# Retention decay put on the values and on a chunk's result, in an attention, routing and FFN kernel on one core

## The chip, the cores and the metric

The kernel runs on one core of a Trainium2 chip. The metric is the device time of one execution in microseconds, lower is better. Three executions of the kernel before took 1035.68, 1039.04 and 1039.63 us, a median of 1039.04 us.

## What is computed

Three layers follow each other. The first is attention with a decaying state, for 4 batches, 8 heads, 768 tokens and a head size of 64; gamma differs from head to head:

```
gamma = 1.0 - 2.0 ** (-5.0 - arange(H))
for t in range(S):
    state = gamma * state + k[t] outer v[t]
    y[t] = (1 / sqrt(D)) * q[t] @ state
```

The second gives each of the 3072 rows to one of 8 experts (384 rows each, by a gate product with `w_gate` and a greedy order over all logits) and applies `relu(x @ w1) @ w2` of that expert. The third is `softplus(x @ w_in) @ w_out`.

## The kernel before

**Stages.** From 0 to about 128 us runs the attention (class `Attn`), with the gate's logits beside it; then the routing of the first expert (class `Route`), until about 164 us; then the two FFN layers expert by expert (class `Ffn`), to the end. The change touches the attention and what is interleaved with it; routing and FFN keep their code.

**Chunks.** The attention works on 24 chunks of 128 tokens, six to a batch. In a chunk no token loop is left: the decay is written as powers of gamma. For a chunk j with place c in its batch (c = j mod 6), TensorE does, in this order within iteration j of `emit`:

- `qk(j+1)` (line 125): scores of the next chunk, keys against queries, into `pA`. VectorE then multiplies `pA` by the table `cm` and writes `at` (line 126). `cm` holds the causal mask, 0.125 and gamma to the power of the distance within a chunk, a plane of its own for each head: 128x1024.
- `xo(j-1)` (line 164): transposes the result `yT` of the chunk before and takes its product with `w_gate`, in one matmul against `rx` (an identity matrix beside the gate's columns), into `pX`. ScalarE copies the rows to `xs` (line 168), SyncE stores them to `xd` (line 178), VectorE sums the gate's parts (`gate`, line 173).
- `y(j)`: where c > 0, the decayed queries `qs` against the state `sb` (line 138), and in all chunks the values against `at` (line 142), both into `pY`. ScalarE copies `pY` to `yT` (line 145).
- `kv(j)` (line 155): where c < 5, the keys against the decayed values `vh`, added into the state `pS`. ScalarE copies it to `sb` (line 157).

`scale` (line 106) makes `qs` on GpSimd: the queries times the table `gqt`, which is loaded in five pieces of 256 KB, one ahead of the queries of each of the chunks 1 to 5 (line 98). `scale_v` (line 114) makes `vh` on ScalarE: eight products, one for each head, with a power of gamma that falls with t; where c = 5 it makes none.

**Interleaved work.** `Conv` turns `w_in` into a high and a low part (16 tiles of 512 KB). Each tile takes three ScalarE instructions (lines 241, 243, 269), three of VectorE (256, 258, 264) and two of GpSimd (242, 259). `side(j, part)` is called three times in an iteration and says how many of its 50 steps shall be done by then; before, this starts in chunk 1, and `cv.ahead()` issues four raw tiles ahead of the loop. After every sixth chunk `R.first_part` puts a list of 12 short VectorE instructions (lines 383 to 399) into the loop, the routing's first look at six chunks of logits.

**What sets the order.** The order is written out by hand in `emit`; each engine takes its instructions strictly in program order. All the big loads are on SyncE's queue in program order: queries with keys (`qk_t`, 512 KB a chunk, four buffers), keys with values (`kv_t`, the same), raw tiles (five buffers), and the stores of `xd`. A load waits until its buffer's last reader is done and, as the queue's rows name it, for an earlier transfer with the same semaphore lane. The PSUM tiles `pA`, `pY`, `pX` have one buffer each: `qk(j+2)` can't write `pA` before `at` of chunk j+1 is made.

Of the kernel before, what the change touches and what calls it, by code (L numbers as in the profile page):

```python
# [20 lines left out]
def shape_tables(H, S):  # L21


    g = 1.0 - 2.0 ** (-5.0 - np.arange(H, dtype=np.float64))
    i = np.arange(128)
    t = i[:, None] + 128 * np.arange(S // 128)
    gk = g ** (-t[:, :, None].astype(np.float64))
    m = np.where(i[:, None] <= i, 0.125 * g[:, None, None] ** (i - i[:, None]).clip(0), 0.0)
    m = m.reshape(H // 2, 2, 128, 128).transpose(2, 1, 0, 3).reshape(128, -1)
    tab = np.concatenate([np.eye(128), m, gk.reshape(128, -1)], axis=1)  # L30
    gq = 0.125 * g[:, None] ** np.arange(S, dtype=np.float64)
    gq = np.repeat(gq.reshape(H // 2, 2, 1, S // 128, 128), 64, axis=2)
    gq = gq.transpose(1, 2, 3, 0, 4).reshape(128, -1)
    return tab.astype(np.float32), gq.astype(np.float32)
# [19 lines left out]
class Attn:  # L54
# [4 lines left out]
    def __init__(self, tc, ctx, ps, qk, kv, w_gate, tab, gqt, ident, L, xd, B, H, S):  # L59
# [34 lines left out]
    def load(self, j, which=("qk", "kv")):  # L94
        for n in (which,) if isinstance(which, str) else which:
            t = self.t[n, j] = self.ld.tile([128, 2, 512], FT, name=n + "_t", bufs=4)
            if n == "qk" and 0 < j < self.NC:
                self.nc.sync.dma_start(self.gq[:, j - 1], self.gq_in[:, j * 512:(j + 1) * 512])
            self.nc.sync.dma_start(t, (self.qk_in if n == "qk" else self.kv_in)[j])

    def scale(self, j):

        c, nc = j % self.NC, self.nc
        if c:
            qs = self.t["qs", j] = self.wk.tile([128, self.HP, 128], FT, name="qs", bufs=2)
            nc.gpsimd.tensor_mul(qs.rearrange("p a t -> p (a t)"), self.t["qk", j][:, 0], self.gq[:, c - 1])

    def scale_v(self, j):

        c, nc = j % self.NC, self.nc  # L110
        if c < self.NC - 1:
            vh = self.t["vh", j] = self.wk.tile([128, self.H, 64], FT, name="vh", bufs=2)
            for h in range(self.H):
                nc.scalar.activation(vh[:, h], self.t["kv", j][:, 1, h * 64:h * 64 + 64], AF.Copy,
                                     scale=self.gk[:, c, h:h + 1])
# [12 lines left out]
    def y(self, j):  # L128
        nc, c = self.nc, j % self.NC
        pY = self.ps.tile([128, 2, 512], FT, name="pY")  # L130
        at, v = self.t["at", j], self.t["kv", j][:, 1]
# [12 lines left out]
        yT = self.t["yT", j] = self.wk.tile([128, 2, 2, 128], FT, name="yT")  # L144
        nc.scalar.activation(yT, pY[:, :, 0:256].rearrange("p b (k t) -> p b k t", k=2), AF.Copy)
# [13 lines left out]
    def xo(self, j):  # L159
# [7 lines left out]
        xs = self.wk.tile([128, 2, 2, 128], FT, name="xs", bufs=3)  # L167
        nc.scalar.activation(xs, pv[:, :, :, 0:128], AF.Copy)
        self.t["xs", j] = xs
        self.t["pv", j] = pv  # L170

    def gate(self, j):
        self.nc.vector.tensor_reduce(self.L[:, j, :], self.t.pop(("pv", j))[:, :, :, 128:136].rearrange("p b a e -> p e b a"),
                                     axis=AX.XY, op=OP.add)
# [6 lines left out]
    def emit(self, side, logits):  # L181
# [3 lines left out]
        self.scale(1)  # L185
        self.late_constants()
        for j in range(n):
# [5 lines left out]
            side(j, 0)  # L193
            if j:
                self.xo(j - 1)
            self.y(j)
            side(j, 1)
            if j:
                self.gate(j - 1)
# [3 lines left out]
            if j + 2 < n:  # L203
                self.scale(j + 2)
# [7 lines left out]
        self.gate(n - 1)  # L212
# [8 lines left out]
class Conv:  # L221
# [673 lines left out]
def model(ctx, tc, qk, kv, w_gate, w1, w2, w_in, w_out, tab, gqt, out, B, H, S):  # L895
# [31 lines left out]
    cv.ahead()  # L927
# [44 lines left out]
```

## Time and profile before

| | us |
|---|---|
| median of three executions | 1039.04 |
| the profiled execution's own time | 1039.39 |
| its span, first to last instruction | 1037.6 |
| TensorE busy | 994.5 (96%) |
| VectorE busy | 636.3 (61%) |
| ScalarE busy | 585.0 (56%) |
| GpSimd busy | 186.1 (18%) |
| bytes read and written in HBM | 83.73 and 12.58 MB |

The shares are means over stages with different limits, so a stage is read by the view of its stretch and by what ended the waits there. L125 is line 125 of the kernel above; a row of the timeline gives the start, the duration, the engine, the line, the operation with its tiles, how many were merged, and in brackets the idle time ahead of it and what ended it. TensorE's matmuls in float32 are shown as two records each, so 8 matmuls read as x16.

### The profile page before, as it was taken

The numbers are of one execution on the slowest core, as the hardware profiler recorded it, in microseconds if no ns is written. First come the engines' busy times: TensorE is split into PE (matmuls) and PEld (weight loads), VectorE is DVE, ScalarE is ACT, GpSimd is POOL, SyncE is SP. The second block draws the span as 40 slices with busy tenths as digits, with TensorE's granted clock in tenths as the row PEclk, the third lists the DMA queues.
The fourth block names the chain that finished last, engine by engine and source line by source line (L and its number), as shares of the span: only waits on it lengthen the run. The fifth ranks groups of instructions, "written<-read, shape, count | busy, mean of one in ns | idle before, by whom it ended". The sixth has DMA issues, their size and how long they took to land.

```text
span 1037.6 us, 19094 instructions
## 1 busy us (share of the span) xinstructions
PE 994.5 (96%) x7266; PEld 901.9 (87%) x7266; DVE 636.3 (61%) x1649; ACT 585.0 (56%) x1245; POOL 186.1 (18%) x204
## 2 busy tenths in 40 slices
PE   5999878999999999999999999999999999999997
PEld 4888757978899889988998889888989899999996
DVE  3686687888766666766575567555665644454432
ACT  4897723676645563566446644665356546654664
POOL 4685422556210101010101010100010020001001
PEclk9998999999999999999999999999999999999999
DMA  9998434423141104110321023101410160014000
GB/s 358 401 405 306 146 96 137 128 82 112 54 142 32 31 21 124 50 31 11 117 67 32 11 92 92 31 1 52 122 32 1 52 192 1 1 41 123 1 1 31
DMA packets 41179, 97.55 MB, mean 94 GB/s; under 512 B 5376, under 2 KB 5504, under 8 KB 41088
## 3 DMA queue, kind: packets, MB, share of 16 engines
q1 hardware_dynamic: 36432, 83.12, 24.1%
q0 software_dynamic: 3840, 12.59, 3.7%
q8 instruction: 57, 0.93, 0.4%
q10 hardware_dynamic: 816, 0.63, 0.2%
q14 instruction: 34, 0.28, 0.1%
HBM read 83.73 MB, written 12.58 MB: 93 GB/s over the span
## 4 chain that ended last, share of the span: by engine, by line
PE 72%; issue 12%; POOL 5%; DVE 5%; DMA 2%; ACT 2%; another core or an unknown queue 0%; SPq 0%; ACTq 0%; POOLq 0%
PE h L659 11%; PE h L662 11%; PE h L660 10%; PE acc L757 7%; PE acc L762 7%; PE acc L758 7%; PE acc L651 3%; PE acc L653 3%; PE acc L652 3%; PE pX L164 2%; POOL wol L259 2%; PE pA L125 2%; POOL cA L242 2%; PE pY L142 2%; PE rt L406 2%
## 5 line engine op out<-in xcount | busy, mean ns | idle before, releaser
L723 DVE SCALAR_TENSOR_TENSOR gf<-h,sp 128x384 f32<-128x384 f32 x128 | 71.2, 556 | 185.2 <-ACT sp L721 185.0
L659 PE MATMUL h<-x2h,wih 128*128 128x384 f32 x512 | 176.5, 345 | 2.0 <-DVE xl L647 2.0
L660 PE MATMUL h<-x2h,wil 128*128 128x384 f32 x512 | 173.3, 338 | 0.0
L757 PE MATMUL acc<-whi,gh 128*128 128x512 f32 x384 | 153.2, 399 | 0.0
L758 PE MATMUL acc<-wlo,gh 128*128 128x512 f32 x384 | 151.2, 394 | 0.0
L719 ACT ACTIVATE sp<-h 128x384 f32<-128x384 f32 x128 | 62.6, 489 | 137.5 <-PE h L662 127.2
L643 ACT ACTIVATE h1h<-h 128x384 fp32r<-128x384 f32 x64 | 31.5, 492 | 148.8 <-PE h L662 105.5
L770 POOL DMA_INDIRECT out_dram<-rows,ix x24 | 25.3, 1053 | 501.4 <-ACT rows L768 498.0
L662 PE MATMUL h<-x2l,wih 128*128 128x384 f32 x512 | 112.8, 340 | 0.8 <-DVE x2l L647 0.6
L762 PE MATMUL acc<-whi,gl 128*128 128x512 f32 x384 | 111.2, 396 | 0.8 <-DVE gl L737 0.8
L659 PEld LDWEIGHTS h<-x2h,wih 128*128 128x128 f32 x512 | 96.6, 189 | 5.8 <-DVE xl L647 2.2
L660 PEld LDWEIGHTS h<-x2h,wil 128*128 128x128 f32 x512 | 96.6, 189 | 3.4
L662 PEld LDWEIGHTS h<-x2l,wih 128*128 128x128 f32 x512 | 92.1, 189 | 2.9 <-DVE x2l L647 2.9
L637 DVE TENSOR_TENSOR wlo<-wraw,whi 128x512 fp32r<-128x512 f32 x128 | 86.3, 689 | 6.1 <-ACT whi L636 6.1
L659 PE MATMUL h<-xh,whi 128*128 128x384 f32 x256 | 89.0, 348 | 0.7 <-ACT xh L646 0.7
L637 DVE TENSOR_TENSOR wlo<-wol,whi 128x512 fp32r<-128x512 f32 x128 | 89.0, 698 | 0.9 <-ACT whi L636 0.9
L651 PE MATMUL acc<-h1h,whi 128*128 128x384 f32 x256 | 88.4, 345 | 0.0
L762 PEld LDWEIGHTS acc<-whi,gl 128*128 128x128 f32 x384 | 72.0, 188 | 18.6 <-DVE gl L737 1.4
L660 PE MATMUL h<-xh,wlo 128*128 128x384 f32 x256 | 86.8, 339 | 0.0
L636 ACT ACTIVATE whi<-wraw 128x512 fp32r<-128x512 f32 x128 | 76.6, 624 | 17.1 <-DMA wraw<-in_moe_w_dram 14.2
L653 PE MATMUL acc<-h1l,whi 128*128 128x384 f32 x256 | 86.1, 336 | 0.0
L652 PE MATMUL acc<-h1h,wlo 128*128 128x384 f32 x256 | 86.1, 336 | 0.0
(201 smaller groups left out, 1932.1 us busy)
## 6 DMA issues: line engine op xcount, KB each, us to landing
wraw<-in_moe_w_dram SPq DMA_DIRECT2D x128, 256.0 KB, 2.7
qk_t<-in_qk_dram SPq DMA_DIRECT2D x24, 512.0 KB, 8.8
kv_t<-in_kv_dram SPq DMA_DIRECT2D x24, 512.0 KB, 6.4
raw<-in_moe_w_in_dram SPq DMA_DIRECT2D x16, 512.0 KB, 7.0
raw<-in_moe_w_out_dram SPq DMA_DIRECT2D x32, 256.0 KB, 2.8
xd<-xs SPq DMA_DIRECT2D x24, 256.0 KB, 4.7
gqt<-in_gqt_dram SPq DMA_DIRECT2D x5, 256.0 KB
ctab<-in_tab_dram ACTq DMA_DIRECT2D x1, 536.0 KB
```

Of the source, the lines that this page charges most:

```text
L636: nc.scalar.activation(hi, raw, AF.Copy)
L637: nc.vector.tensor_tensor(lo, raw, hi.bitcast(FT), op=OP.subtract)
L651: nc.tensor.matmul(ps, wh, ah, start=start, stop=False)
L652: nc.tensor.matmul(ps, wl, ah, start=False, stop=False)
L653: nc.tensor.matmul(ps, wh, al, start=False, stop=stop)
L659: mm(ps, wh(d), ah[:, d], start=d == 0, stop=False)
L660: mm(ps, wl(d), ah[:, d], start=False, stop=False)
L662: mm(ps, wh(d), al[:, d], start=False, stop=d == 3)
L723: nc.vector.scalar_tensor_tensor(g, ps, 0.0, a, op0=OP.max, op1=OP.add)
L757: nc.tensor.matmul(ps, gh[:, s], wh, start=f == 0, stop=False)
L758: nc.tensor.matmul(ps, gh[:, s], wl, start=False, stop=False)
L762: nc.tensor.matmul(ps, gl[:, s], wh, start=False, stop=f == 15)
```

## The change

The decay is split another way. With t = 128 c + i, gamma^(t-s) is gamma^(128 c) gamma^i on a row of the result times gamma^(-s) on a row of the values.

- The scores are multiplied by a plain causal mask, one 128x128 plane read for all eight heads, instead of the eight planes of `cm`. The table loaded with it shrinks from 1072 to 176 columns.
- `vh` is used for the product with `at` too, and is made for every chunk (c = 5 included), with three buffers instead of two.
- The queries go into the state product as they were loaded; `scale`, `qs` and the five loads of `gqt` are gone.
- The copy of `pY` to `yT` becomes a product with a table of factors, on VectorE instead of ScalarE. A table of 532 columns is loaded once; from it VectorE makes the factors of the chunks 1 to 5 with four instructions each, in the iterations before they are used.
- The gate's sum stands ahead of the copy of the rows, and `xo(j-1)` ahead of the first `side` of an iteration.
- No raw tile of `w_in` is issued ahead of the loop. Four are issued one by one, at the three `side` calls of chunk 1 and the first of chunk 2; the steps start in chunk 3 and are spread over the 63 calls from there.

```diff
-    m = np.where(i[:, None] <= i, 0.125 * g[:, None, None] ** (i - i[:, None]).clip(0), 0.0)
-    tab = np.concatenate([np.eye(128), m, gk.reshape(128, -1)], axis=1)
...
+    tab = np.concatenate([np.eye(128), i[:, None] <= i, gk.reshape(128, -1)], axis=1)
+    gq = np.concatenate([gs.reshape(128, -1), (0.125 * gb[:, :, None] ** i).reshape(128, -1)], axis=1)
...
+        self.gb = c.tile([128, gqt.shape[1]], FT, name="gqb")
         self.load(0, "qk")
         nc.scalar.dma_start(ct, tab[:, 128:])
+        nc.scalar.dma_start(self.gb, gqt)
         self.load(0, "kv")
...
-            if n == "qk" and 0 < j < self.NC:
-                self.nc.sync.dma_start(self.gq[:, j - 1], self.gq_in[:, j * 512:(j + 1) * 512])
...
-    def scale(self, j):
-        c, nc = j % self.NC, self.nc
-        if c:
-            qs = self.t["qs", j] = self.wk.tile([128, self.HP, 128], FT, name="qs", bufs=2)
-            nc.gpsimd.tensor_mul(qs.rearrange("p a t -> p (a t)"), self.t["qk", j][:, 0], self.gq[:, c - 1])
+    def factors(self, c):
+        n = (self.NC - 1) * 4
+        if 0 < c < self.NC:
+            for i in range(4):
+                s, k = slice(i * 128, i * 128 + 128), (c - 1) * 4 + i
+                self.nc.vector.tensor_scalar(self.gq[:, c - 1, s], self.gb[:, n:][:, s], self.gb[:, k:k + 1], None,
+                                             op0=OP.mult)
+        return self.gq[:, c - 1] if c else self.gb[:, n:]
...
-        if c < self.NC - 1:
-            vh = self.t["vh", j] = self.wk.tile([128, self.H, 64], FT, name="vh", bufs=2)
+        vh = self.t["vh", j] = self.wk.tile([128, self.H, 64], FT, name="vh", bufs=3)
...
-        nc.vector.tensor_mul(at, pA, self.cm)
+        nc.vector.tensor_tensor(at.rearrange("p s a t -> p (s a) t"), pA.rearrange("p s a t -> p (s a) t"),
+                                self.cm[:, None, :].to_broadcast([128, self.H, 128]), op=OP.mult)
...
-                    nc.tensor.matmul(to(hp, s), self.sb[j % 2][r, hp, :], self.t["qs", j][r, hp, :],
+                    nc.tensor.matmul(to(hp, s), self.sb[j % 2][r, hp, :], qt[r, hp, :],
...
-            nc.tensor.matmul(to(hp, s), v[:, h * 64:h * 64 + 64], at[:, s, hp, :],
+            nc.tensor.matmul(to(hp, s), vh[:, h], at[:, s, hp, :],
...
-        nc.scalar.activation(yT, pY[:, :, 0:256].rearrange("p b (k t) -> p b k t", k=2), AF.Copy)
+        nc.vector.tensor_tensor(yT, pY[:, :, 0:256].rearrange("p b (k t) -> p b k t", k=2),
+                                self.factor[c].rearrange("p (b k t) -> p b k t", b=2, k=2), op=OP.mult)
...
+        nc.vector.tensor_reduce(self.L[:, j, :], pv[:, :, :, 128:136].rearrange("p b a e -> p e b a"),
+                                axis=AX.XY, op=OP.add)
+        xs = self.t["xs", j] = self.wk.tile([128, 2, 2, 128], FT, name="xs", bufs=3)
         nc.scalar.activation(xs, pv[:, :, :, 0:128], AF.Copy)
...
     def side(j, part):
-        if j:
-            cv.step((3 * j - 2 + part) * 50 // 69)
+        n = 3 * j + part
+        if n >= 3:
+            cv.begin()
+        if n >= 9:
+            cv.step((n - 8) * 50 // 63)
...
-    cv.ahead()
     a.emit(side, logits)
```

How the instructions move is seen at three places. The first is the head of SyncE's queue, before the change (`qk_t` and `kv_t` are a chunk's loads, `gqt` a piece of the old table, `raw` a raw tile of `w_in`):

```order
L99 DMA qk_t<-in_qk_dram 128x1024
L99 DMA kv_t<-in_kv_dram 128x1024
L98 DMA gqt<-in_gqt_dram 128x512
L99 DMA qk_t<-in_qk_dram 128x1024
L99 DMA kv_t<-in_kv_dram 128x1024
L98 DMA gqt<-in_gqt_dram 128x512
L99 DMA qk_t<-in_qk_dram 128x1024
L99 DMA kv_t<-in_kv_dram 128x1024
L230 DMA raw<-in_moe_w_in_dram 128x1024 x4
L98 DMA gqt<-in_gqt_dram 128x512
L99 DMA qk_t<-in_qk_dram 128x1024
```

The same queue with the change:

```order
L98 DMA qk_t<-in_qk_dram 128x1024
L98 DMA kv_t<-in_kv_dram 128x1024
L98 DMA qk_t<-in_qk_dram 128x1024
L98 DMA kv_t<-in_kv_dram 128x1024
L98 DMA qk_t<-in_qk_dram 128x1024
L98 DMA kv_t<-in_kv_dram 128x1024
L98 DMA qk_t<-in_qk_dram 128x1024
L98 DMA kv_t<-in_kv_dram 128x1024
L98 DMA qk_t<-in_qk_dram 128x1024
L228 DMA raw<-in_moe_w_in_dram 128x1024 x2
```

The queries and keys of chunk 3 were the last of these rows, behind three pieces of `gqt` and four raw tiles; now they are the seventh, and the raw tiles come after those of chunk 4.

The second place is ScalarE from the making of `vh` (line 114 before, 115 after) through the two chunks behind it, in the second batch. Before:

```order
L114 ACTIVATE vh<-kv_t,ctab 128x64 x8
L168 ACTIVATE xs<-pX 128x512
L145 ACTIVATE yT<-pY 128x512
L269 ACTIVATE wih<-cA 128x4x128
L157 ACTIVATE sb_169<-pS 128x256
L114 ACTIVATE vh<-kv_t,ctab 128x64 x8
L241 ACTIVATE cA<-raw 128x512
L243 ACTIVATE cB<-raw 128x512
L168 ACTIVATE xs<-pX 128x512
L145 ACTIVATE yT<-pY 128x512
L157 ACTIVATE sb_168<-pS 128x256
```

With the change:

```order
L115 ACTIVATE vh<-kv_t,ctab 128x64 x8
L272 ACTIVATE wih<-cA 128x4x128
L174 ACTIVATE xs<-pX 128x512
L244 ACTIVATE cA<-raw 128x512
L246 ACTIVATE cB<-raw 128x512
L161 ACTIVATE sb_168<-pS 128x256
L115 ACTIVATE vh<-kv_t,ctab 128x64 x8
```

The copy to `yT` has left the queue, and `vh` is now what the line of `y` waits for, not only that of `kv`.

The third place is VectorE around the first list of the routing (its last row is G) and the two products to `at` behind it. Before:

```order
L399 TENSOR_TENSOR G<-kx,thr_85 128x276
L258 TENSOR_SCALAR cA<-cA 128x512
L126 TENSOR_TENSOR at<-pA,ctab 128x1024
L264 TENSOR_TENSOR wil<-cA,wih 128x4x128
L173 TENSOR_REDUCE L<-pX 128x8
L256 SCALAR_TENSOR_TENSOR cB<-raw,cB 128x512
L126 TENSOR_TENSOR at<-pA,ctab 128x1024
```

With the change:

```order
L402 TENSOR_TENSOR G<-kx,thr_85 128x276
L259 SCALAR_TENSOR_TENSOR cB<-raw,cB 128x512
L127 TENSOR_TENSOR at<-pA,ctab 128x1024
L171 TENSOR_REDUCE L<-pX 128x8
L261 TENSOR_SCALAR cA<-cA 128x512
L148 TENSOR_TENSOR yT<-pY,gqt 128x512
L267 TENSOR_TENSOR wil<-cA,wih 128x4x128
L127 TENSOR_TENSOR at<-pA,ctab 128x1024
```

The product to `yT` stands between two products to `at`, behind a step of the conversion; the gate's sum (`L<-pX`) comes right behind `at` and waits for TensorE, where it waited for ScalarE before.

## Rows read from the trace of the kernel before

**Rows 1.** Stages: stretch, length, busy (instructions) by engine, granted clock, DMA share, GB/s
```profile
0.00:26.00 26.00, 14.34 (x158) 13.03 (x159) 8.64 (x31) 12.77 (x36) 10.74 (x23) 0.91 0.96 358
26.00:52.00 26.00, 25.11 (x391) 21.84 (x392) 15.95 (x35) 21.89 (x62) 16.58 (x13) 0.96 1.03 401
52.00:78.00 26.00, 24.15 (x394) 21.19 (x390) 21.12 (x36) 24.77 (x75) 20.77 (x15) 1.00 1.03 406
78.00:104.00 26.00, 24.25 (x343) 21.48 (x344) 15.84 (x24) 18.49 (x53) 14.29 (x11) 0.87 0.85 306
```
**Rows 2.** Timeline of the first chunks, VectorE and TensorE
```profile
8.48 1.23 DVE L126 TENSOR_TENSOR at<-pA,ctab 128x1024 f32<-128x1024 f32 x1 [5.29 <-PE pA L125]
10.24 2.08 PE L125 MATMUL pA<-qk_t 64*128 64x128 f32 x16 [1.80 <-DMA qk_t<-in_qk_dram]
14.76 1.16 PE L125 MATMUL pA<-qk_t 64*128 64x128 f32 x16
22.63 2.08 PE L125 MATMUL pA<-qk_t 64*128 64x128 f32 x16 [3.50 <-DMA qk_t<-in_qk_dram]
```
**Rows 3.** Chain that ended last, in the attention: start, us, what
```profile
29.48 1.09 PE pA L125 x16
...
87.04 1.09 PE pA L125 x16
...
89.26 0.60 PE pY L138 x16
...
90.88 0.46 PE pS L155 x16
91.34 1.09 PE pA L125 x16
...
118.27 1.09 PE pA L125 x16
```
**Rows 4.** Waits from 0 to 190 us: engine line, for whom: total, times, longest
```profile
PE pA L125 <- DVE at L126: 5.8, 3, 3.6
```
**Rows 5.** Timeline around the second list of the routing
```profile
75.09 2.50 POOL L106 TENSOR_TENSOR qs<-qk_t,gqt 128x512 f32<-128x512 f32 x2
75.18 1.20 DVE L394 SCALAR_TENSOR_TENSOR kf<-sg,unas 128x6 f32<-128x6 int32 x1
...
79.75 2.08 PE L125 MATMUL pA<-qk_t 64*128 64x128 f32 x16 [3.59 <-DVE at L126]
```
**Rows 6.** Timeline of the attention's end and the last list, from 127.9 us
```profile
127.90 0.60 ACT L168 ACTIVATE xs<-pX 128x512 f32<-128x512 f32 x1 [1.28 <-PE pX L164]
128.53 0.19 DVE L173 TENSOR_REDUCE L<-pX 128x8 f32<-128x32 f32 x1 [3.38 <-ACT xs L168]
128.75 0.20 DVE L383 TENSOR_REDUCE m<-L 128x6 f32<-128x48 f32 x1
...
130.10 0.17 DVE L394 SCALAR_TENSOR_TENSOR kf<-sg,unas 128x6 f32<-128x6 int32 x1
...
130.51 0.30 DVE L399 TENSOR_TENSOR G<-kx,thr 128x276 bf16<-128x276 f16 x1
```
**Rows 7.** Timeline of ScalarE through one chunk with a whole tile of the conversion
```profile
34.42 0.38 ACT L157 ACTIVATE sb<-pS 128x256 f32<-128x256 f32 x1
34.68 2.01 ACT L114 ACTIVATE vh<-kv_t,ctab 128x64 f32<-128x64 f32 x8
...
38.74 0.59 ACT L145 ACTIVATE yT<-pY 128x512 f32<-128x512 f32 x1
39.22 0.38 ACT L157 ACTIVATE sb<-pS 128x256 f32<-128x256 f32 x1
```
**Rows 8.** Groups by line and shape, 0 to 170 us: busy us, mean ns
```profile
L106 POOL TENSOR_TENSOR qs<-qk_t,gqt 128x512 f32<-128x512 f32 x20 | 27.6, 1388 | 12.4 <-DMA qk_t<-in_qk_dram 9.6 <-issue 1.6 <-PE pY L138 1.2
...
L647 DVE TENSOR_TENSOR xl<-h,xh 128x512 fp32r<-128x512 f32 x3 | 2.1, 692 | 2.1 <-ACT xh L646 2.1
```
**Rows 9.** One line's instructions, line 264: duration in ns, shortest, median, longest
```profile
L264 DVE TENSOR_TENSOR wil<-cA,wih x15: 678/684/1760, 31.8 to 121.2; 128x512 fp32r<-128x512 f32 x15
```

More of the change, by code (lines that the diff above doesn't have):

```diff
@@ L27, in shape_tables @@
     gk = g ** (-t[:, :, None].astype(np.float64))
-    m = np.where(i[:, None] <= i, 0.125 * g[:, None, None] ** (i - i[:, None]).clip(0), 0.0)
-    m = m.reshape(H // 2, 2, 128, 128).transpose(2, 1, 0, 3).reshape(128, -1)
-    tab = np.concatenate([np.eye(128), m, gk.reshape(128, -1)], axis=1)
-    gq = 0.125 * g[:, None] ** np.arange(S, dtype=np.float64)
-    gq = np.repeat(gq.reshape(H // 2, 2, 1, S // 128, 128), 64, axis=2)
-    gq = gq.transpose(1, 2, 3, 0, 4).reshape(128, -1)
+    heads = np.array([[[4 * k + 2 * (s ^ b) + s for k in range(H // 4)] for s in range(2)] for b in range(2)])
+    gb = np.repeat(g[heads.reshape(2, -1)], 64, axis=0)
+    gs = gb[:, None] ** (128.0 * np.arange(1, S // 128))[:, None]
+    tab = np.concatenate([np.eye(128), i[:, None] <= i, gk.reshape(128, -1)], axis=1)
+    gq = np.concatenate([gs.reshape(128, -1), (0.125 * gb[:, :, None] ** i).reshape(128, -1)], axis=1)
     return tab.astype(np.float32), gq.astype(np.float32)
@@ L96, in load @@
             t = self.t[n, j] = self.ld.tile([128, 2, 512], FT, name=n + "_t", bufs=4)
-            if n == "qk" and 0 < j < self.NC:
-                self.nc.sync.dma_start(self.gq[:, j - 1], self.gq_in[:, j * 512:(j + 1) * 512])
             self.nc.sync.dma_start(t, (self.qk_in if n == "qk" else self.kv_in)[j])
-    def scale(self, j):
-        c, nc = j % self.NC, self.nc
-        if c:
-            qs = self.t["qs", j] = self.wk.tile([128, self.HP, 128], FT, name="qs", bufs=2)
-            nc.gpsimd.tensor_mul(qs.rearrange("p a t -> p (a t)"), self.t["qk", j][:, 0], self.gq[:, c - 1])
+    def factors(self, c):
[6 more added lines that the diff above has]
+        return self.gq[:, c - 1] if c else self.gb[:, n:]
     def scale_v(self, j):
         c, nc = j % self.NC, self.nc
-        if c < self.NC - 1:
-            vh = self.t["vh", j] = self.wk.tile([128, self.H, 64], FT, name="vh", bufs=2)
-            for h in range(self.H):
-                nc.scalar.activation(vh[:, h], self.t["kv", j][:, 1, h * 64:h * 64 + 64], AF.Copy,
-                                     scale=self.gk[:, c, h:h + 1])
+        vh = self.t["vh", j] = self.wk.tile([128, self.H, 64], FT, name="vh", bufs=3)
+        for h in range(self.H):
+            nc.scalar.activation(vh[:, h], self.t["kv", j][:, 1, h * 64:h * 64 + 64], AF.Copy,
+                                 scale=self.gk[:, c, h:h + 1])
     def qk(self, j):
@@ L184, in emit @@
         self.scale_v(0)
-        self.scale(1)
         self.late_constants()
+        self.factor = [self.factors(0)]
+        self.factor.append(self.factors(1))
         for j in range(n):
@@ L192, in emit @@
                 self.qk(j + 1)
-            side(j, 0)
             if j:
                 self.xo(j - 1)
+            side(j, 0)
             self.y(j)
             side(j, 1)
-            if j:
-                self.gate(j - 1)
             self.kv(j)
@@ L202, in emit @@
                 self.load(j + 3, "kv")
-            if j + 2 < n:
-                self.scale(j + 2)
+            if j + 2 < self.NC:
+                self.factor.append(self.factors(j + 2))
             if j + 1 < n:
@@ L230, in load, with begin @@
         self.nc.sync.dma_start(raw.rearrange("p n b -> p (n b)"), self.plan[p][0])
+    def begin(self):
+        if self.loaded < min(self.bufs - 1, len(self.plan)):
+            self.load(self.loaded)
+            self.loaded += 1
     def ahead(self, p=0):
```

15 lines of the change are left out of this document (4 added, 11 removed).

## The prediction

> **What bounds the kernel now.** I read the view by stages first. From 26 to 104 us TensorE is busy 24 to 25 of 26 us in each stretch, and the DMA engines are full until 78 us at 401 and 406 GB/s; in 78 to 104 the granted clock is only 0.87 [rows 1]. So the attention is held by TensorE, with the loads close behind, and I look for what TensorE loses there. The chain gives its pace: an undisturbed chunk takes 91.34 - 87.04 = 4.30 us, in which the state product is 0.60 and the state update 0.46; both are missing once in a batch of six [rows 3]. From the scores of chunk 4 (29.48) to those of chunk 23 (118.27) there are 19 chunks, so 19 x 4.30 - 3 x 1.06 = 78.5 us of work. It took 88.8 [rows 3]: **10.3 us are lost in the middle.** Of these, 5.8 are three waits of the scores for VectorE's product `at`, which has to free `pA` [rows 4]. After the longest (3.59 us) the scores' records take 2.08 us against 1.16 for the same 16 elsewhere [rows 2, 5]: TensorE went on at 1.2 GHz instead of 2.4. That chunk took 87.04 - 79.75 = 7.29 us, 3.0 too long [rows 3, 5]. The other 1.5 us are small waits.
>
> The timeline of the start shows the second loss. The scores of chunk 2 begin at 14.76; at 4.30 each, chunk 4 would begin at 23.4, and it begins at 29.48 [rows 2, 3]. Chunk 3 waited 3.5 us for its queries and then ran 2.6 us longer at the low clock (22.63 to 29.48 less 4.30): **6.1 us are lost at the start.**
>
> From 164 us on the FFN runs with the same instructions; I leave it as it is.
>
> **The change, part by part.**
>
> *Loads.* By their shapes (a 128x1024 tile is 0.524 MB), the queue had to move 7.2 MB until the queries of chunk 3 were in: tables 0.63, three pieces of `gqt` 0.79, four raw tiles 2.10, seven chunk loads 3.67. They were in at 22.5 [rows 2]. Now it is tables 0.43 and the seven loads, 4.1 MB. At 0.40 MB per us [rows 1] that is 7.7 us sooner, 14.8 us, when TensorE asks for them at about 18.5. The wait goes, and with it the low clock: 6.1 us. The queries of chunk 1 also have 0.45 MB less ahead of them, 1.1 us; but the scores of chunk 1 need `pA` free, which was at 8.48 + 1.23 = 9.71 against their start at 10.24 [rows 2]. Between 0 and 1.1 I take 0.6. Start: **-6.7**, so chunk 4 begins at 22.8.
>
> What is late next: the raw tiles come later, about one in a chunk. The queries of chunk 9 then stand behind 15.1 MB, so at 22.5 + (15.1 - 7.2) / 0.402 = 42.2, and TensorE wants them at 22.8 + 5 x 4.30 - 1.06 = 43.2. That is 1 us to spare. The last values stand behind 39.0 MB, at 101.6; chunk 23 begins later than that.
>
> *GpSimd.* The 20 products to `qs` go, 27.6 us [rows 8]. GpSimd itself is not waited for, but VectorE's short instructions are held while it runs: an instruction on six elements took 1.20 us right behind the start of two `qs`, and 0.17 with GpSimd idle [rows 5, 6]. The list of 12 takes 130.81 - 128.75 = 2.06 us undisturbed [rows 6]; at 75 us it was much longer, and the product to `at` behind it came 3.59 us late [rows 5].
>
> *VectorE.* It gains 24 products to `yT`. The nearest row is a difference of the same 512 columns out of PSUM, 692 ns [rows 8]; bounds are 0.59, ScalarE's copy now [rows 7], and 0.69; I take 0.69. With `at` 1.23, the gate's sum 0.19 and three conversion steps of at most 0.68 each [rows 2, 6, 9] a chunk with a tile costs 4.15 us, just under TensorE's 4.30. So it hides in most chunks, and the list of 2.06 us does not. Behind a list, `at` ends about 0.6 us late, the gate's sum and so the copy to `xs` follow it, and `vh` behind that reaches the line of `y` up to 0.9 late. I charge 1.5 us a list, for three lists 4.5. The bounds are 0 and what a list costs now, (5.8 + 3.0) / 3 = 2.9. The 20 small products of the factors lie between 0.17 and 0.68 each [rows 6, 9]; four of them in a chunk ahead of the conversion, beside `at`, `yT` and the sum (2.1 of 4.30 us): nothing. The mask read for all heads at once leaves `at` its 1024 columns: nothing, and if it were slower, VectorE's 0.15 us would be gone.
>
> *ScalarE.* It loses 24 copies (0.48 from start to start) and gains four `vh` of 2.0 us [rows 7]: -3.5 us in sum. In a chunk with a whole tile it took 39.22 - 34.42 = 4.80 us; without the copy 4.32 [rows 7], as much as TensorE. What is new is a wait: `y` needs `vh`, about 1.0 us ahead of `kv`, which needed it before (89.86 to 90.88 [rows 3]). Behind it in TensorE's queue stand `kv`, the next scores, everything. And `xs` now waits for the gate's sum. Bounds: nothing, or 1.0 us for each of 16 tiles. Most of it lies in the chunk's slack; with other small waits I take 1.0 in all, beside the lists.
>
> *The end.* The gate's sum of the last chunk started 0.63 us after the copy it waited for [rows 6]; it can now start instead of the copy: **-0.6**.
>
> *Sum.* The middle loses 4.5 + 1.0 = 5.5 instead of 10.3: **-4.8**. In all -6.7 - 4.8 - 0.6 = -12.1 us. Against the profiled execution's own 1039.39 that is 1027.3; the median of the runs is 0.35 lower. **I predict 1027 us**, with 1023 to 1031 as this case's own range (0 to 2.9 us a list).
>
> **The rivals.**
>
> *No waits left.* Without `qs` the lists stay short and the slack takes them in. For it: the wait of 3.59 us had two `qs` under it. Against: VectorE has 0.15 us to spare in a chunk with a tile. The 5.5 us go: 1021.5.
>
> *ScalarE sets the pace.* 4.32 against 4.30, and its copy of the rows now hangs on VectorE. If 0.4 us are lost at each of 16 tiles, 6.4 more: about 1033. Against: in the middle stretch it was busy 24.8 of 26 us with the copies still in it [rows 1], and no wait of TensorE was long.
>
> *The loads set the pace.* For it: 1 us to spare at chunk 9. If the rate were that of the first stretch, 358 GB/s [rows 1], the queries of chunk 23 would come at about 110 us instead of TensorE's 106.8 in my sum: 3.2 more, about 1030. Against: 52 us at over 400. The Trainium skill (DMA: Bandwidth & Descriptors, Where 436 GB/s comes from) says that about 358 GB/s of HBM per core bind between HBM and SBUF. By that the sum would be this rival's; the two full stretches at 401 and 406 say otherwise, and the measurement decides.
>
> *Slower: VectorE held by GpSimd becomes the bound.* Two GpSimd instructions a tile remain. Line 264 took 678 ns at best and 1760 at worst [rows 9], 1.08 us of holding. Should two of a tile's three steps be held so, 2.16 us less the 0.15 to spare go on TensorE's path, 2.0 x 16 = 32 us, and the kernel takes about 1059. It decides from 0.9 us of holding a tile on (0.15 + 12.1 / 16). Against: the median of that line was 684 ns with GpSimd busier than it will be. The Trainium skill (SBUF — State Buffer, Who interferes with whom) says that a VectorE instruction with two SBUF inputs is blocked for the whole of a GpSimd instruction that reads SBUF and started first. The 1.20 us row agrees; the median says that few start so.
>
> *No gain.* The new waits eat what the start gives; within 5 us of before.
>
> **How the numbers follow.** Forecast 0.62, no waits 0.14, ScalarE 0.12, loads 0.04, slower 0.05, no gain 0.03. A measurement can tell about 0.5%, 5.2 us. A third of ScalarE's case lies above 1033.8, so faster is 0.62 + 0.14 + 0.04 + 0.08 = 0.88, same 0.04 + 0.03 = 0.07, slower 0.05. The range takes in the case without waits and ScalarE's up to 1033: 1020.5 to 1033.
>
> **What would show it.** Right: the scores of chunk 3 start near 18.5 us without a wait for their load; no stretch between 15 and 110 us at the low clock; the last transposition ends near 116 us instead of 127.9; the three lists last 2 to 3 us and leave waits of 1 to 2 us; the gate's last sum follows TensorE. Wrong: TensorE's line 145 of the new kernel waiting for `vh` in most chunks, line 168 for `yT`, or the scores for their load beyond chunk 8; a second stretch at 0.87; or line 267 with a median well above 0.7 us.

## The result, and the profile after

The changed kernel takes 1027.09 us (median of 1025.20 to 1028.19), against 1038.85 for the kernel before on the same chip: a ratio of 0.9899, with a 95% interval of 0.9874 to 0.9924. The profiled execution's span is 1026.0 us; it was 1037.6. So 11.8 us are saved by the medians and 11.6 by the spans, where 12.1 had been summed up.

The first view is again that by stages, from 0 to 104 us (stretch, busy and instructions by engine in the order PE, PEld, DVE, ACT, POOL, granted clock, DMA share, GB/s):

```profile
0.00:26.00 26.00, 19.84 (x282) 17.76 (x282) 14.16 (x51) 13.13 (x42) 2.73 (x17) 1.00 0.95 358
26.00:52.00 26.00, 25.59 (x388) 21.64 (x388) 23.77 (x49) 24.65 (x76) 17.46 (x12) 1.00 1.03 414
52.00:78.00 26.00, 24.61 (x388) 20.99 (x382) 21.19 (x44) 23.21 (x73) 13.10 (x10) 1.00 1.03 412
78.00:104.00 26.00, 24.35 (x396) 21.44 (x388) 22.14 (x43) 23.08 (x70) 12.99 (x9) 1.00 0.89 334
```

Against [rows 1], TensorE is busy 19.8 us in the first stretch instead of 14.3, and the granted clock is 1.00 in all four, where it had been 0.91, 0.96 and 0.87 in the first, second and fourth. VectorE's load from 26 us on is 21 to 24 us a stretch, where it was 16, 21 and 16; GpSimd's fell there most in the stretch of the second list, from 20.8 to 13.1.

The scores on TensorE's timeline (start, us, engine, line, tiles, in brackets the idle time ahead and what ended it) answer to [rows 2, 5]: chunks 0, 1, 2, 3, 4 and 21.

```profile
4.71 2.08 PE L126 MATMUL pA<-qk_t 64*128 64x128 f32 x16 [4.71 <-DMA qk_t<-in_qk_dram]
8.23 2.08 PE L126 MATMUL pA<-qk_t 64*128 64x128 f32 x16 [1.45 <-DMA qk_t<-in_qk_dram]
...
13.00 1.21 PE L126 MATMUL pA<-qk_t 64*128 64x128 f32 x16
...
17.35 1.16 PE L126 MATMUL pA<-qk_t 64*128 64x128 f32 x16
21.65 1.16 PE L126 MATMUL pA<-qk_t 64*128 64x128 f32 x16
...
97.46 1.16 PE L126 MATMUL pA<-qk_t 64*128 64x128 f32 x16 [1.65 <-DVE at L127]
```

Chunk 3 no longer waits for its load, and chunk 4 begins at 21.65 us. The scores of chunk 23 begin at 106.06. The waits of 0 to 190 us (engine, tile and line, for whom: total, times, longest):

```profile
ACT xs L174 <- DVE L L171: 6.5, 5, 2.7
PE pA L126 <- DMA qk_t<-in_qk_dram: 6.2, 2, 4.7
PE pA L126 <- DVE at L127: 2.9, 3, 1.6
PEld pY L145 <- ACT vh L115: 2.6, 13, 0.3
PE pX L168 <- DVE yT L148: 2.3, 3, 1.7
```

The waits of the scores for `at` fell from 5.8 to 2.9 us [rows 4]. The new waits are there too: `xs` for the gate's sum, `y` for `vh` (13 of them, none above 0.3 us), and the transposition for `yT`.

In the kernel before, the same view (TensorE's timeline) has the scores of the chunks 4 and 23 and the last transposition so:

```profile
29.41 1.16 PE L125 MATMUL pA<-qk_t 64*128 64x128 f32 x16
...
118.20 1.16 PE L125 MATMUL pA<-qk_t 64*128 64x128 f32 x16
...
126.67 1.19 PE L164 MATMUL pX<-rx,yT 128*128 128x136 f32 x8 [0.76 <-ACT yT L145]
```

The chain of [rows 3], on which the prediction's sum rests, sets the two scores 0.07 us later (29.48 and 118.27). From here on both kernels are read by the timeline. By starts of the scores and of the last list's first instruction, the 11.6 us divide up as follows (before: the rows above and [rows 6]).

| stretch | before | after | difference | predicted |
|---|---|---|---|---|
| start to the scores of chunk 4 | 29.41 | 21.65 | -7.8 | -6.7 |
| chunk 4 to chunk 23 | 88.79 | 84.41 | -4.4 | -4.8 |
| scores of chunk 23 to the last list | 10.55 | 10.67 | +0.1 | -0.6 |
| the last list to the end of the span | 908.9 | 909.3 | +0.4 | 0 |

### The profile page after: what moved, and what is told of

It reads as the page before. It is cut to its first block, busy times and chain, and to the rows that moved or that the text cites. A ratio compares the mean times of both kernels' runs of the same rounds, so it can differ in the third digit from the quotient of the medians.

```text
span 1026.0 us, 19093 instructions
## 1 busy us (share of the span) xinstructions
PE 991.6 (97%) x7266; PEld 898.2 (88%) x7266; DVE 646.8 (63%) x1693; ACT 580.8 (57%) x1253; POOL 159.4 (16%) x184
## 4 chain that ended last, share of the span: by engine, by line
PE 66%; issue 13%; POOL 5%; DVE 3%; ACT 1%; DMA 0%; another core or an unknown queue 0%; POOLq 0%
PE h L662 11%; PE h L665 11%; PE h L663 10%; PE acc L760 7%; PE acc L765 7%; PE acc L761 7%; PE acc L654 3%; PE acc L656 3%; PE acc L655 3%; POOL wol L262 2%; POOL cA L245 2%; PE rt L409 2%; PE h L686 1%; POOL out_dram L773 1%; POOL rows L675 0%
## 5 line engine op out<-in xcount | busy, mean ns | idle before, releaser
L773 POOL DMA_INDIRECT out_dram<-rows,ix x24 | 25.2, 1051 | 501.5 <-ACT rows L771 498.0
```

## The experiments

Times are medians with the ratio to the kernel before on the same chip. The next columns give the scores of chunk 4, the stretch from there to chunk 23, and the start of the last list in the profiled execution.

| kernel | us | ratio, 95% interval | chunk 4 at | 4 to 23 | last list at |
|---|---|---|---|---|---|
| before | | | 29.41 | 88.8 | 128.75 |
| changed | 1027.09 | 0.9899 [0.9874, 0.9924] | 21.65 | 84.4 | 116.73 |
| `changed_again` | 1027.89 | 0.9909 [0.9885, 0.9933] | 21.47 | 84.4 | 116.50 |
| `raws_first` | 1032.24 | 0.9955 [0.9938, 0.9971] | 24.56 | 84.4 | 119.58 |
| `late_raws_alone` | 1036.31 | 0.9983 [0.9972, 0.9995] | 24.47 | 90.3 | 125.09 |
| `eight_planes` | 1029.48 | 0.9923 [0.9898, 0.9948] | 23.29 | 84.4 | 118.32 |
| `copy_first` | 1030.76 | 0.9936 [0.9917, 0.9955] | 21.61 | 86.6 | 119.60 |
| `pool_products` | 1034.86 | 0.9972 [0.9958, 0.9987] | 22.12 | 93.2 | 126.00 |
| `yt_scalar` | 1028.43 | 0.9928 [0.9908, 0.9948] | 22.27 | 88.2 | 120.27 |
| `conv_early` | 1025.23 | 0.9889 [0.9868, 0.9911] | 21.07 | 84.3 | 115.24 |
| `spread_lists` | 1022.04 | 0.9854 [0.9832, 0.9877] | 21.03 | 81.6 | 113.29 |
| `spread_early` | 1021.72 | 0.9865 [0.9840, 0.9889] | 22.15 | 81.5 | 113.52 |
| `spread_early_again` | 1021.94 | 0.9851 [0.9827, 0.9875] | 20.98 | 82.3 | 113.17 |

The start of chunk 4 scatters by about 1 us between the kernels with the same start (20.98 to 22.15), so stretches are compared where a difference is below that. The stretch behind the attention, from the last list to the end of the span, scatters more: in the profiled executions it takes 905.5 to 909.3 us, though its code is the same. So what an edit is worth in the attention is read from the stretches, and a median can show some us more or less. (`yt_scalar` computes other values, so only the times of its attention count.)

### The start: raw tiles ahead of the loop

```diff
+    cv.ahead()
     a.emit(side, logits)
```

> The changed kernel with its first four raw tiles of w_in issued ahead of the loop again, all else as changed. My theory (the raw tiles ahead of the queries of chunk 3 are what cost the start): 2.10 MB more stand ahead of them, at 0.41 MB per us 5.1 us later, so they come at about 20 to 21 us where TensorE wants them at 17.3: a wait of about 3 us, and about 2.5 more where TensorE goes on at 1.2 GHz after it. Chunk 4 begins 4 to 6 us later than 21.65, the time is 1031 to 1033, the middle and the end stay. Rival (the smaller tables and the missing pieces of gqt give the start its gain): the queries are in time, chunk 4 begins within 1 us of 21.65, the time is 1027 to 1028.

```profile
20.26 1.16 PE L126 MATMUL pA<-qk_t 64*128 64x128 f32 x16 [3.06 <-DMA qk_t<-in_qk_dram]
24.56 1.16 PE L126 MATMUL pA<-qk_t 64*128 64x128 f32 x16
```

These are the scores of chunks 3 and 4 on its timeline. The wait is there as expected, 3.06 us, so the rival falls. The low clock isn't: the records behind the wait last 1.16 us, and chunk 4 follows 4.30 later. Chunk 4 begins 2.9 us later than in the changed kernel, not 4 to 6; all the rest is as it was, and the last list starts 2.9 later. The time, 1032.24 us, lies in the 1031 to 1033 expected, but is 5.2 us above the changed kernel's median. The two profiled executions lie 2.85 us apart (1030.61 and 1027.76), as the trace shows; for the other 2.3 it shows no cause.

The same part put alone into the kernel before (the diff leaves out `Conv.begin` and the place of `xo`):

```diff
...
 def side(j, part):
-    if j:
-        cv.step((3 * j - 2 + part) * 50 // 69)
+    n = 3 * j + part
+    if n >= 3:
+        cv.begin()
+    if n >= 9:
+        cv.step((n - 8) * 50 // 63)
...
-    cv.ahead()
     a.emit(side, logits)
```

> The kernel before, with the raw tiles issued one by one from chunk 1, the conversion from chunk 3, and xo ahead of the first side call, as in the change; decay, tables, qs and yT as before. My theory: 5.1 MB instead of 7.2 stand ahead of the queries of chunk 3, so they come at about 17.3 to 18 us and the wait and the low clock behind it go: chunk 4 begins at 23 to 24 us instead of 29.5 (-5.5 to -6.5). The three lists still leave waits of 5 to 6 us in sum with a low clock behind the longest, since GpSimd's qs and the rest are as before; about 1032 to 1034. Rival (the start's gain needs the smaller tables too): chunk 4 begins at 26 to 29 us, 1035 to 1039. Second rival (the middle's gain is a later start of the conversion and not the missing qs): the waits of the lists shrink to 3 us here, no low clock after them, and the time is 1027 to 1029.

```profile
15.12 1.90 PE L125 MATMUL pA<-qk_t 64*128 64x128 f32 x16
20.16 1.16 PE L125 MATMUL pA<-qk_t 64*128 64x128 f32 x16
24.47 1.16 PE L125 MATMUL pA<-qk_t 64*128 64x128 f32 x16
```

Those are the scores of chunks 2, 3 and 4. Wait and low clock of chunk 3 are gone, and chunk 4 begins 4.9 us sooner than before, a little less than expected: from chunk 2 to chunk 3 it takes 5.04 us instead of 4.30. The middle is no better, 90.3 us, and the scores' waits for `at` are 5.9 us in sum with the longest 3.8; behind that one the next chunk takes 5.87 us. So the later start of the conversion is not what improved the middle, and the second rival falls. The first rival's time came (1035 to 1039), but not its start (26 to 29 us). Of the 4.9 us part is given back in the middle: the last list starts 3.7 us sooner than before. The medians differ by 1.6 us (1036.31 and 1037.89), where the executions scatter by 2.3 us for this kernel and 6.3 for the one before; so the gain is smaller than expected by any of these numbers.

### The start: the table of eight planes

```diff
-    tab = np.concatenate([np.eye(128), i[:, None] <= i, gk.reshape(128, -1)], axis=1)
+    tab = np.concatenate([np.eye(128), np.tile(i[:, None] <= i, 8), gk.reshape(128, -1)], axis=1)
...
-        nc.vector.tensor_tensor(at.rearrange("p s a t -> p (s a) t"), pA.rearrange("p s a t -> p (s a) t"),
-                                self.cm[:, None, :].to_broadcast([128, self.H, 128]), op=OP.mult)
+        nc.vector.tensor_mul(at, pA, self.cm)
```

> The changed kernel with the causal mask loaded as eight equal planes (0.46 MB more on ScalarE's queue) and read plane by plane, as cm was. My theory (the small table lets the loads of chunks 0 and 1 land sooner, which I had priced at 0.6): the scores of chunk 0 start at 5.9 to 6.5 us instead of 4.7, those of chunk 4 1 to 2 us later than 21.65, and the product to at lasts as long as now; +1 to +2 us, 1028 to 1029. Rival (chunk 0 starts sooner because of the missing pieces of gqt on SyncE's queue): chunk 0 within 0.3 us of 4.7 and the time 1027 to 1027.5.

```profile
6.54 2.08 PE L126 MATMUL pA<-qk_t 64*128 64x128 f32 x16 [6.54 <-DMA qk_t<-in_qk_dram]
...
23.29 1.16 PE L126 MATMUL pA<-qk_t 64*128 64x128 f32 x16
```

The scores of chunk 0 go back to where they were before (6.36 in the kernel before), although the table is on ScalarE's queue and the queries on SyncE's. Chunk 4 and the last list are 1.6 us later, the middle is the same. This is the price of the big table. The product to `at` has the same median duration, 1218 ns from 15 to 118 us, with one plane or eight.

### The middle: GpSimd's products put back, with no use

```diff
+            if j + 2 < n and (j + 2) % self.NC:
+                t = self.wk.tile([128, 512], FT, name="qs", bufs=2)
+                self.nc.gpsimd.tensor_mul(t, self.t["qk", j + 2][:, 0], self.gb[:, 20:532])
             if j + 1 < n:
                 self.scale_v(j + 1)
```

> The changed kernel with 20 extra GpSimd products of 128x512 (the queries times a 512-column table), one in a chunk as qs had been, into a tile that nobody reads. My theory (GpSimd's products held VectorE's short instructions and so made the lists long): the second and third list grow by 1 to 3 us each, the waits of the scores for at grow from 2.9 to 5 us or more, with the low clock behind one of them; +3 to +6 us, 1030 to 1033. Rival (the lists' waits come of VectorE's own load, whatever GpSimd does): lists and waits within 0.5 us of the changed kernel's, 1027 to 1028.

```profile
PE pA L126 <- DVE at L127: 8.2, 5, 3.8
```

The waits of the scores for `at` are 8.2 us (here from 17 to 120 us; 2.9 in the changed kernel), and the middle takes 93.2 us, 8.8 more. That is above the 3 to 6 expected, and the rival falls. The scores wait for no load there, so the loads don't make the difference. The third list on the timeline of VectorE and GpSimd shows how:

```profile
97.68 0.19 DVE L389 TENSOR_REDUCE m<-L 128x6 f32<-128x48 f32 x1
97.84 1.27 POOL L265 TENSOR_TENSOR cA<-cA,cB 128x512 int32<-128x512 int32 x1 [1.57 <-DVE cA L264]
97.91 1.27 DVE L390 TENSOR_TENSOR lm<-L,m 128x48 f32<-128x48 f32 x1
...
100.53 2.49 POOL L206 TENSOR_TENSOR qs<-qk_t,gqb 128x512 f32<-128x512 f32 x2
100.62 1.20 DVE L400 SCALAR_TENSOR_TENSOR kf<-sg,unas 128x6 f32<-128x6 int32 x1
101.86 1.19 DVE L401 TENSOR_SCALAR kx<-kf 128x12 f16<-128x12 f32 x1
103.08 0.30 DVE L405 TENSOR_TENSOR G<-kx,thr 128x276 bf16<-128x276 f16 x1
```

Two instructions on 6 and 12 elements last 1.20 and 1.19 us, each beside one of the two extra products, as in [rows 5]. The list takes 103.08 + 0.30 - 97.68 = 5.70 us, the two ahead of it 3.09 and 3.63. In the changed kernel the three lists take 2.06, 2.59 and 3.66 us; there only the conversion's own GpSimd steps are left to hold the second and the third:

```profile
92.17 1.27 POOL L262 TENSOR_TENSOR cA<-cA,cB 128x512 int32<-128x512 int32 x1 [1.72 <-ACT cA L244]
92.23 1.28 DVE L387 TENSOR_TENSOR lm<-L,m 128x48 f32<-128x48 f32 x1
```

### The middle: the sum behind the copy again

```diff
-        nc.vector.tensor_reduce(self.L[:, j, :], pv[:, :, :, 128:136].rearrange("p b a e -> p e b a"),
-                                axis=AX.XY, op=OP.add)
         xs = self.t["xs", j] = self.wk.tile([128, 2, 2, 128], FT, name="xs", bufs=3)
         nc.scalar.activation(xs, pv[:, :, :, 0:128], AF.Copy)
+        nc.vector.tensor_reduce(self.L[:, j, :], pv[:, :, :, 128:136].rearrange("p b a e -> p e b a"),
+                                axis=AX.XY, op=OP.add)
```

> The changed kernel with the gate's sum behind the copy xs again. My theory: at the end the sum waits for ScalarE again, the list starts 0.6 us later; in the loop nothing, since xs is not waited for by TensorE; in sum +0.5 to +0.8 us, 1027.5 to 1028. Rival (the copy that hangs on VectorE delays vh, and makes the waits of y for vh behind the lists): those waits, 2.6 us in sum, shrink to 1 us or less, and the time is 1025.5 to 1026.5.

```profile
DVE L L173 <- ACT xs L172: 15.5, 16, 2.0
PE pA L126 <- DVE at L127: 4.1, 3, 2.2
```

Both expectations fall. The rival's waits of `y` for `vh` do shrink, from 2.6 to 0.7 us, but the time isn't 1025.5 to 1026.5. From 17 to 120 us VectorE stands 15.5 us before the sum, waiting for the copy, and the waits for `at` grow from 2.9 to 4.1 us. The 15.5 us are no loss by themselves: in the changed kernel VectorE stands as long, 15.4 us, before `yT`, waiting for TensorE (4.3 here). The longest comes at the scores of chunk 21, behind the third list (its first row is that of line 386):

```profile
88.48 1.37 DVE L267 TENSOR_TENSOR wil<-cA,wih 128x512 fp32r<-128x512 f32 x1
...
92.58 0.20 DVE L386 TENSOR_REDUCE m<-L 128x6 f32<-128x48 f32 x1
...
98.04 1.86 PE L126 MATMUL pA<-qk_t 64*128 64x128 f32 x16 [2.20 <-DVE at L127]
```

The records of these scores take 1.86 us instead of 1.16, the stretch from 78 to 104 us shows a granted clock of 0.93, and chunk 22 comes 1.6 us late. In all the middle takes 2.2 us more, and chunk 23 to the last list 0.7 more (11.35 against 10.67). Only the 0.7 had been priced.

Of the 2.2 us, 2.1 lie around the third list; the rest of the middle is in sum as long as in the changed kernel, within 0.1. That list starts at 92.58 instead of 92.00 us. Ahead of it a conversion product (line 267) took 1.37 instead of 0.68 us, beside a GpSimd step. So the wait is 0.55 us longer, and 1.6 us at the low clock follow. This is the fastest of the kernel's four executions (1027.29 us; the others took 1030.51 to 1031.31). So the order may cost more in the loop than this trace shows, and why is not shown.

### The place of `yT`

```diff
-        nc.vector.tensor_tensor(yT, pY[:, :, 0:256].rearrange("p b (k t) -> p b k t", k=2),
-                                self.factor[c].rearrange("p (b k t) -> p b k t", b=2, k=2), op=OP.mult)
+        nc.scalar.activation(yT, pY[:, :, 0:256].rearrange("p b (k t) -> p b k t", k=2), AF.Copy)
```

> The changed kernel with yT made by a plain copy on ScalarE, as before the change; the product with the factors of a row is left out, so the rows and the routing get other values and only the attention's times are to be read. It prices yT's place. My theory (both engines are near TensorE's 4.30 us in a chunk with a tile; ScalarE would need 4.8 with the copy, VectorE 3.5 without the product): the lists' waits for at fall to 1 us or less, but ScalarE sets the pace in the 16 chunks with a tile, y waits for vh there, and chunk 4 to 23 takes 85 to 90 us instead of 84.4. Rival (VectorE alone is scarce, ScalarE has room): chunk 4 to 23 takes 80 to 82.5 us, and y waits for vh no more than now.

```profile
26.00:52.00 26.00, 23.78 (x365) 19.88 (x361) 19.34 (x40) 25.71 (x73) 15.93 (x12) 1.00 1.02 402
52.00:78.00 26.00, 24.34 (x372) 20.48 (x374) 19.43 (x38) 25.16 (x77) 13.12 (x10) 1.00 1.01 396
```

As expected, the waits of the scores for `at` all but vanish (0.2 us), but ScalarE's busy time, the fourth in a row, is now 25.7 and 25.2 of 26 us, and the middle takes 88.2 us: 3.8 more. `y` waits for `vh` 25 times, 5.0 us in sum, and the transposition for `yT` 4.8 us. So `yT` belongs on VectorE here.

With `pool_products` this makes four middles. With GpSimd's products it takes 88.8 us where `yT` is on ScalarE (before) and 93.2 where it is on VectorE; without them 88.2 (`yt_scalar`) and 84.4 (changed). So taking the products away gives 0.6 us by itself, and moving `yT` alone costs 4.4; together they save 4.4. Other parts of the edit differ between the first kernel and the rest, so this is a reading of four kernels and not a test of two switches alone.

### The tail, the lists cut up, and both

The edit to the conversion changes one number, and with it the last conversion product comes ahead of the last chunk:

```diff
-            cv.step((n - 8) * 50 // 63)
+            cv.step((n - 8) * 50 // 58)
```

> The changed kernel with the conversion's steps spread over 58 calls instead of 63, so that its last steps lie ahead of the last chunk's yT. My theory (the product yT of the last chunk stood behind the last conversion product on VectorE, which waited for ScalarE): the stretch from the scores of chunk 23 to its last transposition falls from 10.4 us to 9.0 to 9.4; the denser steps cost 0 to 0.7 us more in the middle (84.4 us from chunk 4 to chunk 23); the last list starts 0.5 to 1.4 us sooner than 116.73. Rival (yT would be late anyway, VectorE has other work there): the tail stays at 10.2 to 10.6 and the time at 1027 to 1028.

In the changed kernel the end of the attention reads so on the timeline of ScalarE, VectorE and TensorE:

```profile
113.21 0.62 ACT L272 ACTIVATE wih<-cA 128x512 fp32r<-128x512 f32 x1
113.86 0.69 DVE L275 TENSOR_TENSOR wil<-cA,wih 128x512 fp32r<-128x512 f32 x1 [1.61 <-ACT wih L272]
114.47 0.68 DVE L148 TENSOR_TENSOR yT<-pY,gqt 128x512 f32<-128x512 f32 x1
115.30 1.16 PE L168 MATMUL pX<-rx,yT 128*128 128x136 f32 x8 [1.66 <-DVE yT L148]
116.50 0.19 DVE L171 TENSOR_REDUCE L<-pX 128x8 f32<-128x32 f32 x1 [1.35 <-PE pX L168]
116.73 0.20 DVE L386 TENSOR_REDUCE m<-L 128x6 f32<-128x48 f32 x1
```

`yT` stands behind the last conversion product, which waits 1.61 us for ScalarE's `wih`. With the edit:

```profile
112.98 0.69 DVE L148 TENSOR_TENSOR yT<-pY,gqt 128x512 f32<-128x512 f32 x1 [1.44 <-PE pY L145]
113.81 1.17 PE L168 MATMUL pX<-rx,yT 128*128 128x136 f32 x8 [0.88 <-DVE yT L148]
...
115.24 0.20 DVE L386 TENSOR_REDUCE m<-L 128x6 f32<-128x48 f32 x1
```

`yT` waits for TensorE alone, and the tail to the end of the transposition takes 114.98 - 105.35 = 9.6 us instead of 10.4: 0.8 saved, somewhat less than expected, with the middle unchanged. From the scores of chunk 23 to the last list it now takes 115.24 - 105.35 = 9.89 us, 0.66 less than in the kernel before. The time, 0.9889 with an interval that covers the changed kernel's ratio, can't show so little.

The first three lists cut up (a generator that yields behind each instruction):

```diff
...
     def side(j, part):
         n = 3 * j + part
+        for _ in range(2):
+            if later and next(later[0], 0) == 0:
+                later.pop()
...
     def logits(j):
-        if j % 6 == 5:
+        if j == NCH - 1:
             R.first_part(j - 5, j + 1)
+        elif j % 6 == 5:
+            later.append(R.parts(j - 5, j + 1))
```

> The changed kernel with each of the first three lists of the routing cut up: two of its 12 instructions at each side call, over two chunks, in place of all at once; the last list is as it was. My theory (a list's 2.06 us in one piece makes at late, and VectorE has a little slack in each chunk to take it in pieces): the waits of the scores for at fall from 2.9 us to 1 or less, those of y for vh by about as much, and chunk 4 to chunk 23 takes 80 to 82 us instead of 84.4; the time is 1023 to 1025. Rival (VectorE is full over the whole stretch, so that the list is paid for wherever it stands): the waits come in more and smaller pieces, chunk 4 to 23 takes 83.5 to 85, the time is 1026.5 to 1028.

```profile
PE pX L168 <- DVE yT L148: 2.1, 2, 1.7
PEld pA L126 <- DVE yT L148: 1.9, 2, 1.2
PE pA L126 <- DMA qk_t<-in_qk_dram: 1.6, 2, 1.0
```

From 17 to 120 us no wait of the scores for `at` is left (two of their weight loads, which overlap other work, are put down to VectorE's `yT`), and the middle takes 81.6 us, 2.8 less. What the scores now wait for in the middle are two loads, 1.6 us, of chunks 19 and 20. By the work of 78.5 us, 3.1 are still lost, half of it to the loads. The rival falls: the list is not paid for wherever it stands.

> Both edits together: the lists cut up, and the conversion's steps over 58 calls. My theory, if each holds by itself: -3 us in the middle and -1 in the tail, so the last list starts at 112 to 113.5 us instead of 116.73, 1022.5 to 1024. Rival (the two ask for the same slack of VectorE): no more than the better of the two by itself.

It took 1021.72 us, a little under the range expected: the middle 81.5 and the tail as in `conv_early`, but a start that happened to be 1.1 us later than that of `spread_lists`. So the two add up by their stretches, and by their times can't be told apart. The last pair was run on one chip:

> The changed kernel once more, beside the next on the same chip. My theory and any rival: 0.988 to 0.991 of the kernel before.

> The lists cut up and the conversion over 58 calls, once more, beside the changed kernel on the same chip. My theory: 4 to 6 us under the changed kernel, 0.983 to 0.987 of the kernel before. Rival (the gain seen was a matter of the chip): under 2 us.

The changed kernel came out at 0.9909, this one at 0.9851, 5.95 us lower in the medians (1027.89 and 1021.94), so the rival falls. In the profiled executions its last list starts 3.3 us sooner (113.17 against 116.50); that much the attention shows. Its middle took 82.3 us this time, with one wait of 1.2 us for a load. It beats both kernels.

## Why the prediction was right

The time, the sign and the terms came out as summed up, to 1.1 us each; three steps behind them did not. That the total is as close as 12.1 against 11.6 is in part luck: the start gave 1.1 us more than its term, the middle and the end 0.4 and 0.7 less, and 0.4 more went behind the last list.

**Start, -6.7 predicted, -7.8 measured.** That the loads held chunk 3, and that raw tiles and tables had to go from ahead of it, is shown from both sides: put back into the changed kernel, the raw tiles cost 2.9 us; taken out of the kernel before, along with the later conversion and the place of `xo`, they give 4.9, as the low clock went there with the wait. The 6.1 us charged for wait and low clock came in full: from chunk 2 to chunk 4 it takes 21.65 - 13.00 = 8.65 us instead of 29.41 - 14.76 = 14.65.

What was mis-sized is the term of 0.6 us for the tables and the pieces of `gqt`: the scores of chunk 2 start 14.76 - 13.00 = 1.76 us sooner. `eight_planes` gives 1.6 at chunk 4 for the table alone. The step that failed is the bound by `pA`, which would not be free for the scores of chunk 1 ahead of 9.71: that moment was taken as fixed, but it hangs on the load of chunk 0, which shared the DMA engines with the big table and now lands 1.65 us sooner (4.71 against 6.36). `late_raws_alone` and `eight_planes` have the raw tiles late and the big table both; between them lie 24.47 - 23.29 = 1.2 us, which the missing pieces of `gqt`, the products that waited for them and the rest of the edit have to share. That wasn't tried by itself, and it is no more than the start's scatter.

**Middle, -4.8 predicted, -4.4 measured.** The 5.5 us that should remain are 84.4 - 78.5 = 5.9. Around the three lists they are 0.9 (chunks 8 to 10), 2.3 (14 to 16) and 1.75 us (20 to 21), 1.65 a list where 1.5 was charged; the 0.9 left lie at chunks 6 to 8, and 1.0 was charged for other waits. The mechanism is shown too: putting GpSimd's products back costs 8.8 us here (`pool_products`), the late conversion gives none (`late_raws_alone`). The chain behind a list is as forecast. At the second one the scores of chunk 15 wait 1.01 us for `at`, the copy to `xs` waits 2.0 us for the gate's sum, and `vh` behind it makes the values of `y` take 1.75 us instead of 1.09:

```profile
73.11 1.75 PE L145 MATMUL pY<-at,vh 128*64 128x128 f32 x16
```

Only the length of the third list, 3.66 us, lies outside the 2 to 3 us that were named. (The 7.29 us of the prediction's longest chunk has its end from the chain and its start from the timeline; by the timeline it is 86.97 - 79.75 = 7.22, which changes no term.)

What the sum did not have is how much hangs on `yT` going to VectorE along with it: with `yT` on ScalarE the middle would take 88.2 us, about as much as before. The sum's move was priced at -0.6 and at the end alone. With the gate's sum behind the copy the middle of the profiled execution loses 2.2 of its 4.4 us, so the step "in the loop nothing" is in doubt; but nearly all of it is one late list with the low clock behind, so what the order is worth in the loop stays open. The 0.69 us of `yT` on VectorE was right:

```profile
L148 DVE TENSOR_TENSOR yT<-pY,gqt x20: 679/691/693, 17.0 to 114.5; 128x512 f32<-128x512 f32 x20
L267 DVE TENSOR_TENSOR wil<-cA,wih x15: 681/685/1400, 32.8 to 110.6; 128x512 fp32r<-128x512 f32 x15
```

**End, -0.6 predicted, +0.1 measured.** The gate's part came: from the end of the transposition to the list it takes 116.73 - (115.30 + 1.16) = 0.27 us instead of 128.75 - (126.67 + 1.19) = 0.89. But from the scores of chunk 23 to that end it takes 10.4 us instead of 9.7, since `yT` of the last chunk, now on VectorE, stands behind a conversion product. `yT` had been costed beside the loop's pace alone and not at its last place, where nothing runs behind it to hide it. With the conversion out of its way (`conv_early`) the end takes 0.66 us less than before, the -0.6 of the sum.

**The rivals.** That `y` would wait for `vh` in most chunks was named as a sign of ScalarE setting the pace. It waits 13 times, in 11 of the 24 chunks, for at most 0.3 us each, and undisturbed chunks still take 4.30 us: the sign didn't come, the rival falls. The transposition (line 168) waits for `yT` three times, 2.3 us in sum, of which 1.7 are at the end. The loads ran at 414 and 412 GB/s over 52 us, not at 358, and no scores waited for a load beyond chunk 1; that rival became true only once the lists were cut up. The slower rival needed 0.9 us of holding a tile; the median of line 267 is 685 ns, 1 ns from that of before [rows 9], and the three steps of the 16 tiles ran 3.2 us in sum over 0.68, 0.68 and 0.42 us, so 0.2 a tile.

## What to carry to other kernels

Where one engine sets the pace and another has little slack in each step, cut a periodic block of short instructions into pieces: the same 12 instructions cost 1.65 us a list in one piece, and two at a time they left no wait of the scores for VectorE's product, until the loads became the next limit. When an instruction changes its engine, cost it at the last iteration too, and look at what stands ahead of it there. And where two readers of one result wait for each other, as the gate's sum and the copy of the rows do, try the short one first: that was worth 0.7 us at the end here, and 2.2 in the loop of one execution, mostly at one list. Last, a move that frees one engine and a move that fills another may only pay together: here each by itself left the middle at 88 us or more.

## What had not been expected of the hardware

- A load was delayed by another queue's load from the first microseconds: 0.46 MB more on ScalarE's queue delayed the first load on SyncE's by 1.8 us (4.71 to 6.54). At 0.41 MB per us, the rate of the full stretches, these bytes alone would be 1.1 us.
- Waits of TensorE of like length were followed by either clock: full speed behind 3.06 us (`raws_first`, chunk 3), 1.2 GHz behind 3.50 [rows 2] and, for part of the records, behind 2.20 (`copy_first`, chunk 21). The price of a wait can't be read from its length alone; the 2.5 us charged for it in `raws_first` weren't due.
- VectorE's instructions that read one operand from PSUM were not held by GpSimd at all. In `pool_products`, with the most GpSimd work, these are the durations from 15 to 118 us (shortest, median, longest, ns):

```profile
L148 DVE TENSOR_TENSOR yT<-pY,gqt x18: 678/691/693, 17.5 to 115.0; 128x512 f32<-128x512 f32 x18
L127 DVE TENSOR_TENSOR at<-pA,ctab x22: 1205/1216/1225, 14.7 to 117.7; 128x1024 f32<-128x1024 f32 x22
L270 DVE TENSOR_TENSOR wil<-cA,wih x14: 681/775/1620, 34.3 to 115.6; 128x512 fp32r<-128x512 f32 x14
```

The first two read PSUM and one table in SBUF, and spread by 20 ns at most; the third reads two tiles in SBUF and goes up to 1620. The Trainium skill (SBUF — State Buffer, Who interferes with whom) says that a VectorE instruction with at most one SBUF input, outside the two-port modes, doesn't contend with GpSimd. These rows agree. So a product out of PSUM like `yT` was the right kind of work to move there. One operand in SBUF and none in PSUM didn't spare an instruction: `kx<-kf` above took 1.19 us beside a GpSimd product. Whether it ran in a two-port mode no run here shows.
